# The gate's logits taken ahead of the squares of the value rows

## The chip, the cores and the metric

The kernel runs on one core of a Trainium2 chip. The core has five engines with instruction streams of their own, which meet only through semaphores: TensorE (PE, matrix products), VectorE (DVE), ScalarE (ACT), GpSimd (POOL) and SyncE (SP), whose queue issues nearly all DMA transfers. Each engine takes its instructions strictly in the order in which the program lists them. The metric is the device time of one execution in microseconds; the median of several executions counts.

## The reference

The result mixes two branches by a gate that is computed per token:

```python
x = A_u                                     # 1 x 2048 x 576
g = sigmoid((x * gate_w).sum(-1))           # the gate
a = _A_ref(x, ...)                          # a long convolution by spectra
b = _B_ref(x, w_q, k1, k2, u, v)            # product-key experts
return g * a + (1 - g) * b
```

Branch a builds a filter of 2048 taps for each of 576 channels from a state space of 128 modes and convolves it with x. Branch b scores 2048 tokens by 32 heads against two sets of 64 keys, takes the best two of each, and of their four sums the best two, weighs them with a softmax, and sums for each token the rows of `v` (4096 x 576) with weights `g * gelu(x . u)`.

## The kernel before

The products run in two half-precision parts: every large operand is split into a high and a low float16 part with a common scale, and three partial products are summed. For that the scale must be known first: for the value rows `v` it comes from the sum of their squares.

The program is written as generators, and a planner inside the kernel runs them. It keeps a clock of its own, `clock`, with estimated costs for each engine and for the DMA wire; a generator yields the time after which it wants to be called again, or waits with `ready(...)` until the planner believes that an operand is there. The planner only fixes the order of the instructions; on the chip each waits for what it really needs. So a generator that starts at another planned time, or in another order, changes the order of everything that is planned after it.

The stages, in order: the taps of the filter and, between them, the first scores (`s`, weights `whl`) and activations (`a`, weights `uhl`); `k_stage1`, the first transform of the 32 taps' rows (`k`, 32 pairs of output banks, evicted as `k1o` by ScalarE or VectorE and stored to `sk_d`, at most four tiles `k1o` in flight); `products`, the pointwise products of the spectra (`pr`, `pi`, `vf`, `pv`, `vo`); the last scores, `gating`, the transposes `tr`; the last activations; and then, token tile by token tile in the order 0, 15, 1, 14, ..., the one-hot products `S` (operands `A`, `Bg` from VectorE), their product with the activations' gelu (`gl`), the split of that into `wh`, and the output products `o` with the split value rows `vhl`. The products `s`, `a` and `k` run on the two row halves of the array, an upper and a lower half beside each other.

`v_norm` (L1529) is the generator around which the change lies. It reads 48 blocks of 128 rows through two buffers `vn`. The blocks 0 to 31 are the value rows: one DMA, and a sum of squares on ScalarE (`vj` with `vsum`). Behind block 31 the scale `sv` is formed and `vnormed` is set; `v_work` (L1577) waits for that, and then splits the eight chunks `vhl` of value rows: ScalarE writes the high part, and the low part goes to VectorE in one instruction or, where the planner thinks GpSimd free, over ScalarE and GpSimd. The raw rows of a chunk are loaded into the tile of the next one, so the tiles must be open. The blocks 32 to 47 are x itself: four DMAs (`au_load`), a multiplication by `gate_w` on GpSimd, and a sum on ScalarE (`vj` with `gA`). Behind the last a sigmoid makes the gate of `gA`, and `gates` is set.

`freq` (L1399) spawns `v_norm` 40 us of planned time after it has issued the loads of the spectra tables and taps (`tk`, `ksb`), opens the tiles of the chunks 0 to 2 behind `k_stage1`, of 3 and 4 behind `products`, and of 5 to 7 only when both `gated` (set by the last `gating`) and `gates` are set:

```python
        while not gated or not gates:
            yield 0.5
        FG.__exit__(None, None, None)
        WJ.__exit__(None, None, None)
        v_pool(5, 8)
```

All instructions of the three vector engines are recorded by one line, L136, the DMAs by L207 and the matmuls by L216, so the profile tells them apart by the names of their tiles.

Of the kernel before, what the change touches and what calls it, by code (L numbers as in the profile page):

```python
# [18 lines left out]
AF = mybir.ActivationFunctionType  # L19
# [121 lines left out]
def body(ctx: ExitStack, tc: tile.TileContext, xT, au, par, logdt, dskip, gatew, wq, kT, uT, vv,  # L141
# [56 lines left out]
    S = Engine(nc.scalar, rdy, clock, key, act_cost)  # L198
# [3 lines left out]
    def dma(o, i, q=None):  # L202
        t = max(clock[0], rdy.get(key(i), 0.0), queue[0])
        queue[0] = t + 0.45
        wire[0] = max(wire[0], t) + (2 if o.dtype in (F16, BF16) else 4) * o.shape[0] * size(o) / 3.4e5
        rdy[key(o)] = max(rdy.get(key(o), 0.0), wire[0] + 2.2)
        (q or DQ).dma_start(o, i)  # L207
# [63 lines left out]
    def spawn(gen, after=0.0):  # L271
        heapq.heappush(heap, (clock[0] + after, nseq[0], gen))
        nseq[0] += 1
# [118 lines left out]
    def au_load(a, t):  # L392
        for d, o in au_rows(au, t, a):
            dma(o, d)
# [53 lines left out]
    gA = top.tile([128, NT], F32, name="gA")  # L448
# [950 lines left out]
    def freq():  # L1399
        nonlocal ff, ab, iota_a, iota_b  # L1400
        ff = FG.__enter__()
        wrems.append(ff.tile([128, 2, 512], F16, name="wrem3"))
        ksb = KS.__enter__().tile([128, 4, NCK // 2, 32, 2 * NI], F16, name="ksb")
        fk = FK.__enter__()
        tabs = [fk.tile([128, 16, 2, 128], F16, tag="tk", name=f"tk{w0}", bufs=2) for w0 in (0, 16)]
        for w0, tkt in zip((0, 16), tabs):
            dma(tkt, tk_d[:, w0:w0 + 16, :])
        for j in range(4):
            while wire[0] > clock[0] + 2:
                yield 0.3  # L1410
            dma(ksb[:, j].rearrange("p c w i -> p c (w i)"),
                k_d[:, 32 * j:32 * j + 32].rearrange("c l z m n -> (l z m) c n"))
        spawn(v_norm(), 40)
        spawn(gating(0), 20)
        yield from k_stage1(ksb, fk, tabs)
        FK.__exit__(None, None, None)
        KS.__exit__(None, None, None)
        v_pool(0, 3)
        spawn(v_work())
        fp = FP.__enter__()  # L1420
        quota(sc=4, wb=5)
        yield 3
        yield from products(fp)
        FP.__exit__(None, None, None)
        quota(sc=4, wb=4)
        ab = ctx.enter_context(tc.tile_pool(name="ab", bufs=1, side="right"))
        iota_a = ab.tile([128, 128, 2], F16, name="iota_a")
        iota_b = ab.tile([128, 64, 2], F16, name="iota_b")
        V.tensor_copy(iota_a, cst[:, 384:512, None].to_broadcast([128, 128, 2]))
        V.tensor_copy(iota_b, cst[:, 512:576, None].to_broadcast([128, 64, 2]))  # L1430
        spawn(prep(0))
        v_pool(3, 5)
# [5 lines that stand above are left out]
        shut.append(1)  # L1438
# [87 lines left out]
    vhl, sv, vnormed, gates = [], [], [], []  # L1526
    vt = {}

    def v_norm():  # L1529
        ld = {}  # L1530

        def load(b):
            a = ff.tile([128, D], F32, tag="vn", name=f"vn{b}", bufs=2)
            if b < 32:
                dma(a, vv[128 * b:128 * b + 128])
            else:
                au_load(a, b - 32)
            ld[b] = a

        gw = row(gatew, "gw", ff)  # L1540
        load(0)
        for b in range(48):
            if b + 1 < 48:
                load(b + 1)
            a = ld.pop(b)
            yield from ready(a)
            ju = ff.tile([128, D], BF16, tag="ju", name=f"vj{b}")
            if b < 32:
                S.activation(ju, a, AF.Square, accum_out=vsum[:, b:b + 1])
            else:  # L1550
                G.tensor_mul(a, a, gw)
                yield from ready(a)
                S.activation(ju, a, AF.Copy, accum_out=gA[:, b - 32:b - 31])
            yield 2
            if b != 31:
                continue
            V.tensor_reduce(out=nut[:, 2:3], in_=vsum, axis=AX, op=OP.add)
            yield from ready(nut)
            tag = side()
            yield from need(tag)  # L1560
            p = bank(tag, "pvn")
            mm(p[:, 0:1], onesb, nut.bitcast(BF16)[:, 5:6], True, True, 0.05)
            yield from ready(p)
            sv.extend(root_scale(p[:, 0:1], 1.02))
            free(tag, sv[0], of=p)
            vnormed.append(1)
            del p
        S.activation(gA, gA, AF.Sigmoid)
        gates.append(1)

    def v_pool(c0, c1):

        vp = ctx.enter_context(tc.tile_pool(name=f"vp{c0}", bufs=1, side="right"))
        for c in range(c0, c1):
            vt[c] = vp.tile([128, 4, 2, D], F16, name=f"vhl{c}")
# [458 lines left out]
```

## Time and profile before

| | |
|---|---|
| median of 3 runs | 1461.31 us (1460.85 to 1463.2) |
| the profiled execution | 1463.78 us, of which the span is 1462.0 us |
| TensorE busy | 1426.9 us, 98% of the span |
| VectorE, ScalarE, GpSimd busy | 1199.1, 848.8, 527.5 us |
| granted TensorE clock, mean | 0.991 |
| sums of squares and of the gate on ScalarE (`vj`, 48) | first at 719.2 us, last at 969.9 us |
| sigmoid of the gate | 972.8 us |
| splits `vhl` on ScalarE | 859.7 to 1021.3 us |
| first output product `o` | 996.6 us |

A row of a timeline gives start and duration in us, engine, line, operation, output and inputs, the shape, a count, and in brackets how long the engine idled before and for what. A row of the slices gives the stretch, its length, the busy time of PE, weight load, DVE, ACT and POOL with the number of instructions, the granted TensorE clock (1.00 is full), the busy share of the DMA engines and GB/s. A row of the waits gives who waited for whom, the total in us, how often, and the longest.

### The profile page before, as it was taken

What the parts mean: (1) busy time and instruction counts of PE and PEld (TensorE: products, weight loads), DVE (VectorE), ACT (ScalarE), POOL (GpSimd) and SP (SyncE); (2) the same over time, 40 slices, a digit from 0 to 9 for tenths busy, and PEclk for the clock granted to TensorE, in tenths of its full rate; (3) what the DMA queues carried; (4) which work ended last, traced back from release to release, by engine and by line L of the source; (5) the groups of instructions that cost most, each with busy time, mean ns of one, the idle gap of its engine ahead of it and who ended that gap; (6) DMA issues with size and microseconds to landing.
All of it is one profiled execution on the core that took longest, in us unless ns stands there. A gap on an engine that the chain in (4) does not pass through costs nothing. (4 is left out here: it accounts for less than half of the span.)

```text
span 1462.0 us, 44130 instructions
## 1 busy us (share of the span) xinstructions
PE 1426.9 (98%) x17654; PEld 901.9 (62%) x17654; DVE 1199.1 (82%) x4559; ACT 848.8 (58%) x1477; POOL 527.5 (36%) x515
## 2 busy tenths in 40 slices
PE   7999999999999999999999999999899999999999
PEld 3465566554565565455654444446687887888787
DVE  6888699889889988767899997568998988998860
ACT  6647887987888877754566765755424224223310
POOL 0442266543472663430368899413110110010100
PEclk9999999999999999999999999999999999999999
DMA  9433543333341331248767786767433432442400
GB/s 312 124 112 101 160 126 113 109 122 107 112 147 47 126 103 45 74 146 258 252 253 254 271 287 213 243 195 251 146 101 117 140 120 91 133 148 67 156 10 17
DMA packets 134381, 215.89 MB, mean 148 GB/s; under 512 B 10912, under 2 KB 79904, under 8 KB 127776
## 3 DMA queue, kind: packets, MB, share of 16 engines
q1 hardware_dynamic: 134080, 213.01, 44.9%
q8 instruction: 138, 2.26, 0.6%
q14 instruction: 67, 0.55, 0.1%
q10 hardware_dynamic: 96, 0.07, 0.0%
HBM read 141.74 MB, written 71.30 MB: 146 GB/s over the span
## 5 line engine op out<-in xcount | busy, mean ns | idle before, releaser
L216 PE MATMUL s<-whl,xb 64*128 64x512 f16 x3072 | 466.0, 377 | 0.1
L216 PE MATMUL a<-xb,uhl 64*128 64x512 f16 (+1 forms) x3024 | 458.0, 378 | 0.7 <-ACT uhl L136 0.3
L216 PE MATMUL o<-vhl,wh 128*128 128x288 f16 x3072 | 390.1, 287 | 1.2 <-DVE vhl L136 1.2
L216 PEld LDWEIGHTS <-wh 128*128 128x128 f16 x3072 | 297.0, 98 | 79.5 <-issue 5.5
L216 PEld LDWEIGHTS <-xb 64*128 64x128 f16 x3456 | 222.1, 94 | 167.5 <-issue 14.8
L216 PEld LDWEIGHTS <-uhl 64*128 64x128 f16 (+1 forms) x3024 | 196.4, 94 | 167.0 <-issue 8.9
L136 ACT ACTIVATE wh<-gl,s_wg 128x1024 f16<-128x1024 f32 x64 | 68.9, 1137 | 199.0 <-DVE gl L136 199.0
L136 POOL TENSOR_TENSOR CS<-CS,ex 128x512 f32<-128x512 f32 x72 | 90.7, 1295 | 167.6 <-DVE ex L136 167.6
L136 POOL TENSOR_TENSOR ya<-ya,db 128x576 f32<-128x576 f32 x16 | 32.0, 2011 | 317.2 <-DMA ya<-in_au_dram 158.2
L216 PE MATMUL s<-wrem,xb 64*128 64x512 f16 x384 | 123.1, 376 | 0.0
L216 PE MATMUL a<-xb,wrem 64*128 64x512 f16 (+1 forms) x380 | 120.7, 377 | 0.0
L136 ACT ACTIVATE go<-a,i_a 128x512 f32<-128x512 f32 x100 | 68.4, 685 | 88.0 <-PE a L216 65.3
L136 DVE FIND_INDEX8 i<-m,sx 128x8 uint32<-128x64 f32 x592 | 116.5, 215 | 0.0
L136 DVE TENSOR_TENSOR gl<-S,gl 128x256 f32<-128x256 f32 x256 | 90.3, 414 | 16.4 <-PE S L216 10.0
L136 DVE SCALAR_TENSOR_TENSOR wh<-gl,s_wg,wh 128x1024 f16<-128x1024 f32 x64 | 89.6, 1428 | 14.2 <-ACT wh L136 14.1
L136 POOL TENSOR_TENSOR e<-aN,rt 128x512 f32<-128x512 f32 x72 | 84.0, 1189 | 47.4 <-PE kb L216 47.3
L136 DVE TENSOR_TENSOR Bg<-Be,vals 128x1024 f16<-128x1024 f16 x128 | 88.4, 732 | 2.2
L136 DVE FIND_INDEX8 i<-m,s 128x8 uint32<-128x64 f32 x432 | 87.0, 220 | 0.0
L136 DVE MAX8 m<-sx 128x8 f32<-128x64 f32 x592 | 81.4, 207 | 6.2 <-ACT sx L136 5.9
L136 ACT ACTIVATE gl<-gl 128x1024 f32<-128x1024 f32 x64 | 63.4, 1044 | 33.3 <-DMA gl<-g_d 33.2
L216 PE MATMUL S<-Bg,A 128*128 128x64 f16 x2048 | 74.6, 195 | 7.9 <-DVE Bg L136 7.9
L136 DVE MAX8 m<-s 128x8 f32<-128x64 f32 x432 | 61.7, 214 | 24.2 <-PE s L216 20.0
(209 smaller groups left out, 2468.3 us busy)
## 6 DMA issues: line engine op xcount, KB each, us to landing
g_d<-go SPq DMA_DIRECT2D x128, 256.0 KB, 2.6
gl<-g_d SPq DMA_DIRECT2D x32, 1024.0 KB, 5.4
wq<-in_wq_dram SPq DMA_DIRECT2D x16, 1152.0 KB, 6.1
su_d<-us SPq DMA_DIRECT2D x32, 288.0 KB, 2.6
sk_d<-k1o SPq DMA_DIRECT2D x32, 288.0 KB, 3.0
vn<-in_vv_dram SPq DMA_DIRECT2D x32, 288.0 KB, 5.2
ui<-su_d SPq DMA_DIRECT2D x16, 576.0 KB, 4.2
ki<-sk_d SPq DMA_DIRECT2D x16, 576.0 KB, 5.4
```

The lines of the kernel that those rows point to most:

```text
L136: return f(*a, **k)
L216: return T.matmul(o, l, r, start=start, stop=stop)
```

## The change

In `v_norm` the blocks are taken in the order 32 to 47, then 0 to 31; the sigmoid and `gates` stand behind block 47, the scale still behind block 31, which is now the last. `freq` spawns the generator 4 instead of 40 us of planned time after its own loads.

```diff
-        spawn(v_norm(), 40)
+        spawn(v_norm(), 4)
...
         gw = row(gatew, "gw", ff)
-        load(0)
-        for b in range(48):
-            if b + 1 < 48:
-                load(b + 1)
+        order = [*range(32, 48), *range(32)]
+        load(32)
+        for n, b in enumerate(order):
+            if n + 1 < 48:
+                load(order[n + 1])
             a = ld.pop(b)
...
             yield 2
+            if b == 47:
+                S.activation(gA, gA, AF.Sigmoid)
+                gates.append(1)
             if b != 31:
                 continue
...
-        S.activation(gA, gA, AF.Sigmoid)
-        gates.append(1)
```

The order of the instructions moves with it from the tap stage on. The first place is SP's queue at the start of `k_stage1`, behind the loads of the taps `ksb`; `k1o` with a number is the evicted tile of that tap, `vn32` and on are the blocks of x. Before:

```order
L207 DMA ksb_11201<-k_d_68 128x18x256 x3
L207 DMA sk_d_67<-k1o0_11703 32x4x576
L207 DMA sk_d_67<-k1o1_11706 32x4x576
L207 DMA sk_d_67<-k1o2_11758 32x4x576
L207 DMA sk_d_67<-k1o3_11772 32x4x576
L207 DMA sk_d_67<-k1o4_11827 32x4x576
L207 DMA sk_d_67<-k1o5_11840 32x4x576
```

and now:

```order
L207 DMA ksb_11201<-k_d_68 128x18x256 x3
L207 DMA gw_11647<-in_gatew_dram 128x576
L207 DMA vn32_11649<-in_au_dram 32x576 x4
L207 DMA vn33_11654<-in_au_dram 32x576 x4
L207 DMA sk_d_67<-k1o0_11715 32x4x576
L207 DMA vn34_11839<-in_au_dram 32x576 x4
L207 DMA sk_d_67<-k1o1_11718 32x4x576
L207 DMA sk_d_67<-k1o2_11772 32x4x576
L207 DMA vn35_11902<-in_au_dram 32x576 x4
L207 DMA sk_d_67<-k1o4_11851 32x4x576
L207 DMA sk_d_67<-k1o3_11787 32x4x576
```

Fourteen of the sixteen blocks of x, four DMAs each, and the row of `gate_w` now stand among the 32 stores of that stage, where that row and six value-row blocks, one DMA each, stood.

The second place is VectorE's order just ahead of its first work on the products `S15_0` of the second token tile (`gl15_0<-S15_0`). Before:

```order
L136 TENSOR_TENSOR Bg15_0_17192<-Be15_0_17190,vals_80 128x1024 x2
L136 TENSOR_TENSOR A115_1_17195<-iota_a_16322,vals_80 128x2048
L136 TENSOR_TENSOR Be15_1_17197<-iota_b_16323,vals_80 128x1024
L136 TENSOR_TENSOR Bg15_1_17199<-Be15_1_17197,vals_80 128x1024 x2
L136 SCALAR_TENSOR_TENSOR vhl4_16330<-vhl5_17144,sci_76,vhl4_16330 128x576 x2
L136 SCALAR_TENSOR_TENSOR vhl5_17144<-vhl6_17145,sci_76,vhl5_17144 128x576
L136 TENSOR_SCALAR go7_1_2_17422<-a7_1_2_17311,i_a_91 128x512
L136 TENSOR_SCALAR go7_2_3_17427<-a7_2_3_17277,i_a_91 128x512
L136 TENSOR_TENSOR gl15_0_17184<-S15_0_0_17388,gl15_0_17184 128x32x8
```

and now:

```order
L136 TENSOR_TENSOR Bg15_0_17228<-Be15_0_17226,vals_80 128x1024 x2
L136 TENSOR_TENSOR A115_1_17231<-iota_a_16476,vals_80 128x2048
L136 TENSOR_TENSOR Be15_1_17233<-iota_b_16477,vals_80 128x1024
L136 TENSOR_TENSOR Bg15_1_17235<-Be15_1_17233,vals_80 128x1024 x2
L136 SCALAR_TENSOR_TENSOR vhl6_16491<-vhl7_16492,sci_76,vhl6_16491 128x576
L136 SCALAR_TENSOR_TENSOR vhl7_16492<-vs_17160,sci_76,vhl7_16492 128x576
L136 TENSOR_SCALAR go7_2_3_17362<-a7_2_3_17278,i_a_91 128x512
L136 SCALAR_TENSOR_TENSOR vhl7_16492<-vs_17160,sci_76,vhl7_16492 128x576
L136 TENSOR_TENSOR gl15_0_17220<-S15_0_0_17383,gl15_0_17220 128x32x8
```

The last splits of value rows, of the chunks 6 and 7, now stand ahead of `S15_0`; before, the chunks 4 and 5 stood there.

The third place is VectorE's order later in the same passage, up to its first work on `S1_0` of the third token tile (`gl1_0<-S1_0`). Before:

```order
L136 SCALAR_TENSOR_TENSOR wh15_1_17662<-gl15_0_17184,s_wg_92,wh15_0_17661 128x1024
L136 SCALAR_TENSOR_TENSOR vhl6_17145<-vhl7_17146,sci_76,vhl6_17145 128x576
L136 SCALAR_TENSOR_TENSOR wh15_1_17662<-gl15_0_17184,s_wg_92,wh15_0_17661 128x1024
L136 SCALAR_TENSOR_TENSOR ya0_17523<-y0_0_0_17759,iuk_94,ya0_17523 128x288
L136 SCALAR_TENSOR_TENSOR ya0_17523<-y0_0_1_17764,iuk_94,ya0_17523 128x288
L136 SCALAR_TENSOR_TENSOR wh15_1_17662<-gl15_1_17185,s_wg_92,wh15_0_17661 128x1024
L136 SCALAR_TENSOR_TENSOR vhl7_17146<-vs_17540,sci_76,vhl7_17146 128x576
L136 SCALAR_TENSOR_TENSOR wh15_1_17662<-gl15_1_17185,s_wg_92,wh15_0_17661 128x1024
L136 SCALAR_TENSOR_TENSOR ya15_17528<-y0_1_0_17769,iuk_94,ya15_17528 128x288
L136 SCALAR_TENSOR_TENSOR ya15_17528<-y0_1_1_17774,iuk_94,ya15_17528 128x288
L136 SCALAR_TENSOR_TENSOR vhl7_17146<-vs_17540,sci_76,vhl7_17146 128x576 x2
L136 TENSOR_TENSOR gl1_0_17664<-S1_0_0_17826,gl1_0_17664 128x32x8
```

and now:

```order
L136 TENSOR_TENSOR A11_1_17657<-iota_a_16476,vals_80 128x2048
L136 TENSOR_TENSOR Be1_1_17659<-iota_b_16477,vals_80 128x1024
L136 TENSOR_TENSOR Bg1_1_17661<-Be1_1_17659,vals_80 128x1024 x2
L136 SCALAR_TENSOR_TENSOR wh15_1_17644<-gl15_0_17220,s_wg_92,wh15_0_17643 128x1024 x2
L136 SCALAR_TENSOR_TENSOR wh15_1_17644<-gl15_1_17221,s_wg_92,wh15_0_17643 128x1024 x2
L136 SCALAR_TENSOR_TENSOR ya0_17554<-y0_0_0_17751,iuk_94,ya0_17554 128x288
L136 SCALAR_TENSOR_TENSOR ya0_17554<-y0_0_1_17756,iuk_94,ya0_17554 128x288
L136 TENSOR_TENSOR gl1_0_17646<-S1_0_0_17777,gl1_0_17646 128x32x8
```

The splits of the chunks 6 and 7 have left this place, and the combinations of `ya15` stand further behind.

## Prediction

> **What bounds the kernel now.** I read the busy shares of the page first, then who TensorE waited for, then the span in slices of 10 us, then TensorE's timeline at the few gaps.
>
> ```profile
> PE 1426.9 (98%) x17654; PEld 901.9 (62%) x17654; DVE 1199.1 (82%) x4559; ACT 848.8 (58%) x1477; POOL 527.5 (36%) x515
> PE S L216 <- DVE Bg L136: 7.9, 6, 3.1
> PE k L216 <- ACT k1o L136: 2.4, 2, 2.2
> PE k L216 <- DVE m L136: 1.9, 1, 1.9
> PE tr L216 <- DVE vals L136: 1.2, 1, 1.2
> PE o L216 <- DVE vhl L136: 1.2, 1, 1.2
> ```
>
> TensorE (PE) is busy for 1426.9 of 1462.0 us, so all that a reordering can win is in 35 us of gaps. The change removes no matmul. What it can move is the waits listed (total us, times, longest), and these lie in two places: the stage of the tap transforms (`k`, 684 to 730 us) and the passage from the activations `a` to the one-hot products `S` and the output products `o` (915 to 1040 us). Slices of that passage (PE busy, PEld, DVE, ACT, POOL, then the granted clock):
>
> ```profile
> 920.00:930.00 10.00, 9.96 (x116) 5.60 (x117) 3.70 (x16) 6.88 (x19) 2.63 (x2) 0.66 0.92 306
> 950.00:960.00 10.00, 7.78 (x80) 3.63 (x78) 9.44 (x19) 3.05 (x7) 1.42 (x1) 0.83 0.35 95
> 1000.00:1010.00 10.00, 10.00 (x118) 8.18 (x117) 9.93 (x23) 2.40 (x4) 0.94 (x1) 0.84 0.76 204
> 1030.00:1040.00 10.00, 6.16 (x55) 4.43 (x55) 9.93 (x19) 0.42 (x1) 0.00 (x0) 0.70 0.01 2
> ```
>
> A gap costs twice: after it the granted clock falls. The same instructions at both clocks (start, duration, idle before):
>
> ```profile
> 920.04 0.31 PE L216 MATMUL tr<-identb,vals 128*64 128x64 bf16 x4 [1.23 <-DVE vals L136]
> 954.09 0.20 PE L216 MATMUL S<-Bg,A 128*128 128x64 f16 x1 [1.82 <-DVE Bg L136]
> 954.69 1.31 PE L216 MATMUL S<-Bg,A 128*128 128x64 f16 x31 [0.40 <-DVE Bg L136]
> 961.97 2.12 PE L216 MATMUL a<-xb,uhl 64*128 64x512 f16 x18
> 991.21 1.14 PE L216 MATMUL S<-Bg,A 128*128 128x64 f16 x32
> 999.24 0.19 PE L216 MATMUL S<-Bg,A 128*128 128x64 f16 x1 [1.75 <-DVE Bg L136]
> 1001.47 4.67 PE L216 MATMUL o<-vhl,wh 128*128 128x288 f16 x30
> 1015.86 2.15 PE L216 MATMUL y<-yz,tf 128*32 128x288 f32 x32
> 1017.94 3.85 PE L216 MATMUL o<-vhl,wh 128*128 128x288 f16 x30
> 1034.86 0.23 PE L216 MATMUL S<-Bg,A 128*128 128x64 f16 x1 [3.14 <-DVE Bg L136]
> 1035.46 1.81 PE L216 MATMUL S<-Bg,A 128*128 128x64 f16 x31 [0.37 <-DVE Bg L136]
> 1037.08 5.63 PE L216 MATMUL o<-vhl,wh 128*128 128x288 f16 x30
> ```
>
> 32 `S` take 1.14 us and 30 `o` 3.85 us at the full clock; behind the 3.14 us gap they take 1.81 and 5.63, some 2.5 us more.
>
> The Trainium skill, "TensorE: Matmul & The Clock Gate", section "HAM oscillation — how this bites in real kernels", says that only idle gaps above about 3.4 us cost clock. Here the trace differs: 1.23 us of idle stands ahead of a slice granted 0.66, 1.82 us ahead of none but within one granted 0.83. By the page the slow clock in the second term below (0.8 us) would be none of the wait's doing, and the sum 2.8 us instead of 3.6; I go by the rows.
>
> **The change, part by part.** *The squares' end and VectorE's part of the value rows.* The order of VectorE shows the remaining value-row splits (`vhl`) ahead of the first product of the second token tile, `S15_0`, where before six stood behind it, among the work on which `S15_2` and `S1_2` wait. Their prices, and what GpSimd adds to them:
>
> ```profile
> 1004.10 0.81 DVE L136 SCALAR_TENSOR_TENSOR vhl<-vhl,sci,vhl 128x576 f16<-128x576 f32 x1
> 1010.37 1.28 POOL L136 TENSOR_TENSOR vhl<-vhl,vhl 128x576 f16<-128x576 f32 x1 [9.43 <-ACT vhl L136]
> 1010.48 3.53 DVE L136 TENSOR_TENSOR Bg<-Be,vals 128x1024 f16<-128x1024 f16 x2
> 1018.45 2.16 POOL L136 TENSOR_TENSOR vhl<-vs,vhl 128x576 f16<-128x576 f32 x1 [3.19 <-ACT vs L136]
> 1019.39 1.83 DVE L136 SCALAR_TENSOR_TENSOR vhl<-vhl,sci,vhl 128x576 f16<-128x576 f32 x1
> 1028.63 0.93 DVE L136 SCALAR_TENSOR_TENSOR ya<-y,iuk,ya 128x288 f32<-128x288 f32 x2
> 1038.50 1.29 DVE L136 TENSOR_TENSOR Bg<-Be,vals 128x1024 f16<-128x1024 f16 x2
> ```
>
> VectorE was at 9.93 of 10 us in the slices at 1000 and 1030, so there it sets the pace. Gone from its chain between `S15_0` and `S1_2`: six splits at 0.81, 4.9 us; two `ya` combinations that now stand behind, 0.93; and the stretching of its instructions while GpSimd works on `vhl` (a `Bg` pair at 3.53 instead of 1.29, a split at 1.83 instead of 0.81; some of the first is due to another GpSimd instruction), of which I count half of 2.2 and the whole 1.0, 2.1 us. Together 7.9 us. But the order also draws `S1_2` forward: 156 `o` stand ahead of it instead of 192, 36 × 3.85/30 = 4.6 us less cover, against 8 more `a` matmuls, whose pair costs 2.12/9 = 0.24 at most and 0.22 from start to start: 0.9. Net 7.9 − 4.6 + 0.9 = 4.2 us of gain. Bounds: nothing, if the splits that moved forward make `S15_0` late instead (the slice at 920, with VectorE at 3.70 of 10, speaks against it), and 10 us, which is all that TensorE lost from `S15_0` at 991.2 to 1034.9 (43.7 us elapsed; 192 `o` at 0.123, six groups of `S` at 1.07, the 32 `y` at 2.1 and 14 `a` make 33.6).
>
> The Trainium skill, "SBUF — State Buffer", section "SBUF: two separate sides", says that VectorE and GpSimd share one port pair as an exclusive lock, the loser waiting out the whole instruction. By it the 1.28 and 2.16 us would return in full, 3.4 instead of my 2.1; the row of 3.53 us agrees with such a stop.
>
> *The first products.* Between `S0_1` and `S0_2` stand 50 `a` matmuls instead of 36: 14 × 0.11 = 1.5 us more cover for waits of 1.82 + 0.40, and with 0.7 us left I let the slow clock behind it go too (the slice at 950 was granted 0.83, 1.7 us of full clock less, and half of that fell on work: 0.8). Gain 2.3; bounds 0 and 3.3.
>
> *The transposes `tr`.* ScalarE no longer has four sums of the gate between its 16 evictions, but VectorE has four splits between them. 19 `a` instead of 11 lie between the transposes, 0.9 us of cover. I take 0.9 of the 1.23; bounds −2 (two of the split pairs on the path) and 4.6 (the wait and the clock of the slice at 920).
>
> *The gate's rows in the tap stage.* Sixteen blocks, each four loads, one multiplication on GpSimd, one sum on ScalarE, move from 842–970 us to behind the load of the taps; 14 of them are issued before the last of the 32 stores of `k1o`, on the same queue, SP. ScalarE runs its queue in order, and 50 of the 64 evictions `k1o` stand on it behind these sums. TensorE has four banks for them, two taps. What a late block does there, the squares showed, which until now began in this stage:
>
> ```profile
> 719.16 0.68 ACT L136 ACTIVATE vj<-vn 128x576 bf16<-128x576 f32 x1 [3.93 <-DMA vn<-in_vv_dram]
> 690.00:700.00 10.00, 9.78 (x120) 7.63 (x116) 5.97 (x42) 6.93 (x21) 2.40 (x8) 1.00 0.72 268
> 700.00:712.00 12.00, 11.98 (x143) 9.08 (x140) 11.09 (x85) 6.43 (x22) 4.18 (x14) 1.00 0.57 214
> 712.00:720.00 8.00, 6.51 (x76) 4.86 (x71) 6.08 (x37) 3.52 (x15) 3.85 (x13) 1.00 0.84 263
> 720.00:730.00 10.00, 9.23 (x101) 6.23 (x102) 8.72 (x60) 6.97 (x23) 1.13 (x4) 1.00 0.85 280
> L136 ACT ACTIVATE k1o<-k x50: 388/411/487, 686.3 to 729.6; 128x288 f32<-128x288 f32 x50
> L207 SPq DMA_DIRECT2D sk_d<-k1o x32: 517/518/1402, 687.0 to 730.0; - x32
> L207 SPq DMA_DIRECT2D vn<-in_au_dram x64: 310/419/1385, 842.1 to 963.7; - x64
> L136 POOL TENSOR_TENSOR vn<-vn,gw x16: 1399/1414/2385, 854.2 to 965.9; 128x576 f32<-128x576 f32 x16
> vn<-in_vv_dram SPq DMA_DIRECT2D x5, 288.0 KB, 4.6
> vn<-in_au_dram SPq DMA_DIRECT2D x22, 72.0 KB, 2.1
> ```
>
> From 712 to 730 us TensorE lost 18 − 15.74 = 2.3 us, and the first sum waited 3.93 us for its rows. That stall goes, since the squares now come after the stage. In its place: two buffers for the rows, so two blocks per round of four issues (4 × 0.42 = 1.7), landing (2.1 in a quiet window, 4.6 in this one), 1.41 on GpSimd and 0.68 + 0.19 on ScalarE: 6.1 to 8.6 us, 3.0 to 4.3 a block. Fourteen blocks in the 43.3 us of the evictions have 3.1 each. So the rows fall behind by up to 14 × 1.2 = 17 us at the worst landing and not at all at the best; the queue itself needs 32 × 0.52 + 56 × 0.42 = 40 of 43 us. I take a landing of 3.2 us, nearer the quiet row because the stage before the squares moved only 0.57 to 0.72 of the DMA time: 7.2 us a round, 0.5 a block over, 7 us in all, less the two taps of slack (2 × 1.4 = 2.8) at the end: about 4.2, against the 2.3 that goes. Cost 1.9. Bounds: a gain of 2.3, and a loss of 12 (17 − 2.8 − 2.3).
>
> *The stage of the products (730 to 915).* It loses 16 multiplications of 1.41 us on GpSimd and gets squares without any, and none of the waits listed at the top falls in it. I leave it at 0; bounds ±2, about what the squares' first block cost in the tap stage. The sigmoid moves ahead of two of the exponentials: as many table loads in the order as before, 43.
>
> *Pairs of row halves.* Counting the halves of the array in TensorE's order, 3684 pairs of full-height-split `s`, `a` and `k` matmuls stand instead of 3694, and 115 singles instead of 96: 9 more passes at 0.22, a cost of 1.9, which nothing hides, since TensorE is the bound.
>
> Sum: 4.2 + 2.3 + 0.9 − 1.9 + 0 − 1.9 = 3.6 us of gain. The profiled execution took 1463.78 us, 1462.0 of them span; it would become 1460.2. It stands 2.5 above the median of the runs, 1461.31, so for the median I say 1457.7, 0.25% faster. About 0.2%, 2.9 us, is what a measurement of this kernel can tell from no change.
>
> **The rivals.** *The tap stage is held by the gate's rows.* Speaks for it: SP at 40 of 43 us by issue alone, and a row that lands in 4.6 us under just this mixture. Against: the two quiet windows. It decides when a landing passes some 4 us: then a round is 8 us, a block 0.9 over, 12.6 in all, TensorE's loss 12.6 − 2.8 − 2.3 = 7.5 instead of 1.9, and the sum −2.0: 1463.3; at 4.6 us it is 1467.8. This is the side of slower.
>
> *The waits only change their place.* VectorE's work between 915 and 1037 us is not less by the change, two splits and three evictions `go` are even more in the order from the transposes to `S1_2`, some 4 us; where it was idle before (3.70 of 10 at 920) it can take them, but if it cannot, the 4.2 of the first term becomes 0.2 and the time 1461.7: no change.
>
> *More goes than I count.* If `tr` and both `S` waits vanish with their slow clock, the first three terms are 10 + 3.3 + 4.6 instead of 7.4, and the time is 1447; half of that is 1452.
>
> **How the numbers follow.** Forecast 0.38 and the larger gain 0.10; no change 0.24; the tap stage 0.28. Faster is 0.48, within 0.2% 0.24, slower 0.28. The forecast's own range is 1454 to 1460. The range for all reaches up to 1467, where the tap stage's bad landing ends, and down to 1450, and leaves out about 2 in 10.
>
> **What would show it.** Right: no wait of `S` on `Bg` above 2.5 us from 990 to 1040 and no `vhl` behind `S15_0` on VectorE; clock at 1030 to 1040 above 0.8. The tap stage: `k` waits for `k1o` above 5 us in total, ScalarE waiting for GpSimd's `vn`, last `k1o` later than 735. Wrong above all: a landing of the gate's rows above 4 us there, or a new wait of `S15_0`.

## The result, and the profile after

The changed kernel took 1460.52 us in the median of 14 runs (1458.07 to 1463.49), the kernel before 1462.12 (14 runs, 1458.90 to 1464.39). The ratio is 0.9991, with a 95% interval of 0.9981 to 1.0000: about a tenth of a per cent, and no change by the bound of 0.2%. The profiled execution took 1462.77 us (span 1461.0) against 1463.78 (span 1462.0) before.

The page of the changed kernel, and who TensorE waited for between 680 and 1100 us (total us, times, longest):

```profile
PE 1427.4 (98%) x17652; PEld 902.7 (62%) x17654; DVE 1196.3 (82%) x4573; ACT 837.1 (57%) x1452; POOL 520.7 (36%) x513
PE S L216 <- DVE Bg L136: 4.4, 6, 1.5
PE k L216 <- ACT k1o L136: 2.0, 4, 1.0
PE pr L216 <- DMA ki<-sk_d: 1.8, 1, 1.8
PE pv L216 <- DVE vo L136: 1.7, 1, 1.7
PE wn L216 <- ACT wj L136: 0.9, 1, 0.9
```

The waits of the late passage are nearly halved (`S` for `Bg` 7.9 to 4.4), those of `tr` and of `o` for `vhl` are gone. In their place stand waits that were not there before: `wn` and `pr` for `ki` at the start of the products, and `pv` at their end. (Before, `pi` and `pr` waited 0.9 us each at 886 to 896; these two are gone.) TensorE's timeline at these places (start, duration, idle before in brackets):

```profile
742.68 0.16 PE L216 MATMUL wn<-sc,onesb 64*128 64x1 bf16 x1 [0.75 <-DVE i L136]
743.97 0.16 PE L216 MATMUL wn<-sc,onesb 64*128 64x1 bf16 x1 [0.90 <-ACT wj L136]
750.89 0.43 PE L216 MATMUL pr<-ki,cst 64*64 64x256 f32 x2 [1.76 <-DMA ki<-sk_d]
...
913.16 1.08 PE L216 MATMUL pv<-vf,cst 64*64 64x256 f32 x4 [1.72 <-DVE vo L136]
963.74 0.20 PE L216 MATMUL S<-Bg,A 128*128 128x64 f16 x1 [0.36 <-DVE Bg L136]
965.41 1.10 PE L216 MATMUL S<-Bg,A 128*128 128x64 f16 x31 [1.48 <-DVE Bg L136]
...
995.57 1.14 PE L216 MATMUL S<-Bg,A 128*128 128x64 f16 x32
...
1003.68 0.20 PE L216 MATMUL S<-Bg,A 128*128 128x64 f16 x1 [1.37 <-DVE Bg L136]
...
1031.10 0.20 PE L216 MATMUL S<-Bg,A 128*128 128x64 f16 x1
1031.69 1.10 PE L216 MATMUL S<-Bg,A 128*128 128x64 f16 x31 [0.39 <-DVE Bg L136]
```

The first product of `S1_2`, which stood behind 3.14 us of idle time at 1034.86, now starts at 1031.10 without a wait (with 36 fewer `o` ahead of it). The slices (PE busy, PEld, DVE, ACT, POOL, granted clock, share of the transfer engines, GB/s; in the last three PE alone):

```profile
712.00:720.00 8.00, 7.02 (x82) 5.02 (x78) 5.37 (x43) 5.81 (x22) 5.88 (x12) 1.00 0.86 278
720.00:730.00 10.00, 9.28 (x107) 6.25 (x104) 7.82 (x50) 5.96 (x19) 6.10 (x14) 1.00 0.82 276
740.00:750.00 10.00, 7.36 (x117) 4.56 (x113) 8.54 (x69) 6.25 (x15) 2.97 (x7) 1.00 0.80 288
750.00:760.00 10.00, 9.11 (x111) 4.38 (x113) 8.08 (x34) 3.50 (x11) 4.93 (x7) 1.00 0.75 242
...
900.00:910.00 10.00, 10.00 (x138) 1.00 1.02 364
910.00:920.00 10.00, 8.28 (x54) 0.66 0.49 176
1030.00:1040.00 10.00, 9.61 (x128) 1.00 0.70 247
```

The two rows of the kernel before:

```profile
740.00:750.00 10.00, 9.75 (x178) 6.01 (x176) 8.45 (x58) 7.59 (x18) 6.09 (x9) 1.00 0.59 210
750.00:760.00 10.00, 10.00 (x106) 4.54 (x102) 9.92 (x68) 5.79 (x15) 9.16 (x16) 1.00 0.73 290
```

At 1030 TensorE is busy 9.61 of 10 us at the full clock (6.16 at 0.70 before). At 740 to 760 it lost 3.5 us (0.25 before); and the clock of 0.66 that stood behind the wait of `tr` at 920 now stands behind the wait of `pv`, one slice earlier.

In the tap stage the rows of the gate land quickly, and the stage is longer nevertheless:

```profile
L136 ACT ACTIVATE k1o<-k x52: 392/411/519, 687.8 to 734.8; 128x288 f32<-128x288 f32 x52
vn<-in_au_dram SPq DMA_DIRECT2D x47, 72.0 KB, 2.4
ACT vj L136 <- POOL vn L136: 6.9, 5, 2.3
```

The last `k1o` on ScalarE comes at 734.8 us instead of 729.6, though a row lands in 2.4 us; ScalarE waited 6.9 us for products of GpSimd.

### The profile page after: what moved, and what is told of

It is laid out like the page before. It is cut to its first block, busy times and chain, and to the rows that moved or that the text cites. A ratio compares the mean times of both kernels' runs of the same rounds, so it can differ in the third digit from the quotient of the medians.

```text
span 1461.0 us, 44118 instructions
## 1 busy us (share of the span) xinstructions
PE 1427.4 (98%) x17652; PEld 902.7 (62%) x17654; DVE 1196.3 (82%) x4573; ACT 837.1 (57%) x1452; POOL 520.7 (36%) x513
## 5 line engine op out<-in xcount | busy, mean ns | idle before, releaser
L216 PEld LDWEIGHTS <-xb 64*128 64x128 f16 x3456 | 226.5, 94 | 167.5 <-issue 14.5
L136 DVE FIND_INDEX8 i<-m,s 128x8 uint32<-128x64 f32 x520 | 104.8, 221 | 0.0
L136 DVE FIND_INDEX8 i<-m,sx 128x8 uint32<-128x64 f32 x504 | 99.3, 217 | 0.0
L136 DVE MAX8 m<-s 128x8 f32<-128x64 f32 x520 | 74.2, 214 | 26.5 <-PE s L216 22.5
L136 DVE TENSOR_TENSOR A<-iota_a,vals 128x2048 f16<-128x2048 f16 x64 | 78.4, 1224 | 0.0
L136 ACT ACTIVATE CS<-CS 128x1024 f32<-128x1024 f32 x72 | 74.6, 1050 | 6.3 <-DVE CS L136 6.1
```

The lines of the kernel that those rows point to most:

```text
L136: return f(*a, **k)
L216: return T.matmul(o, l, r, start=start, stop=stop)
```

## The experiments

My theory after the result: the late passage gained about what was forecast, and the gain was spent in four places: the gate's rows in the tap stage, the start of the products, the end of the products (the loads of the value rows beside the stores `z_d`), and fewer pairs of row halves. The rival: the gain was never there, since VectorE has as much to do as before, and waits only changed place. All runs are compared with the kernel before on the same chip; the median of the kernel before lay between 1461.2 and 1462.1 throughout.

**Six splits less, nothing else moved.** In the kernel before, in its own order:

```diff
-                        V.scalar_tensor_tensor(h[:, j, 1, :], x, sv[0], h[:, j, 0, :], op0=OP.mult, op1=OP.subtract)
+                        if 12 <= len(nsplit) < 18:
+                            V.charge("scalar_tensor_tensor", h[:, j, 1, :], x, sv[0], h[:, j, 0, :], op0=OP.mult, op1=OP.subtract)
+                            nc.vector.memset(h[:, j, 1, :], 0.0)
+                        else:
+                            V.scalar_tensor_tensor(h[:, j, 1, :], x, sv[0], h[:, j, 0, :], op0=OP.mult, op1=OP.subtract)
+                        nsplit.append(1)
```

`charge` tells the planner the cost of the split, so that the order stays; the kernel leaves out the low parts of six blocks of value rows.

> The kernel before, in exactly its order, with six of VectorE's nine splits between S15_0 and S1_2 turned into a fill of the same half tile (their values are left out; 0.81 us each and up to 1.8 beside POOL becomes a fill that reads nothing). This does alone what the largest term of the prediction said of the change. If VectorE's chain sets the end of this passage: the waits of S for Bg, 17 us in six before by sum with clock, fall by 4 us or more and the time is 1456 to 1458.5. If the time removed from VectorE there is only waited for elsewhere (the arrival of loads, ScalarE's copies, the order of TensorE): 1460 to 1462, and the waits change place.

1459.48 us, ratio 0.9981 (0.9971 to 0.9990): faster, with a median between the two expectations. The fills, and three starts of `S`: the first row of `S` is that of `S15_0`, the last that of `S1_2`:

```profile
L1616 DVE MEMSET vhl<- x6: 298/298/298, 978.6 to 1016.8; 128x288 uint32 x6
...
989.03 1.14 PE L223 MATMUL S<-Bg,A 128*128 128x64 f16 x32
...
997.08 0.19 PE L223 MATMUL S<-Bg,A 128*128 128x64 f16 x1 [1.76 <-DVE Bg L136]
...
1031.45 0.20 PE L223 MATMUL S<-Bg,A 128*128 128x64 f16 x1 [3.14 <-DVE Bg L136]
```

Only three of the six fills lie in the passage (at 1002.0, 1004.0 and 1016.8). The other three stand at 978.6 to 979.5, ahead of `S15_0`, and behind them VectorE has nothing to do for 9.7 us. So the run removes less than its expectation says. From `S15_0` to `S1_2` TensorE takes 1031.45 − 989.03 = 42.42 us instead of 43.65, which is 1.2 us less; from VectorE's first eviction `gl` of `S15_0` to `S1_2` it is 40.8 instead of 42.0, also 1.2 less. What VectorE is relieved of there arrives at TensorE one to one. So the passage is paced by VectorE, as the prediction had it, but this run shows it for 1.2 us and not for the 4.2 forecast.

`S1_2` starts 3.4 us earlier than before (1034.86 to 1031.45), but 2.2 of these were there at `S15_0` already (991.21 to 989.03), ahead of all that the fills could do. Most of that is the clock: the slice from 950 to 960, granted 0.83 before, is granted 1.00 here behind the same waits. Of the 2.5 us between the medians the traces place 1.2; where the rest lies is open.

My expectation of the waits was wrong. `S` waits 7.9 us for `Bg` as before, and 3.14 ahead of `S1_2` as before; what went is the wait of `o` for `vhl`, 1.2 us. (The 17 us that the expectations give to the waits of `S` before stand in no view; the waits shown above are 7.9.) A relief of the pacing engine need not show in the wait one looks at.

**Each half of the change alone.** The early start with the old order:

```diff
-        spawn(v_norm(), 40)
+        spawn(v_norm(), 4)
```

> The first half of the change alone: the generator of the value rows starts at +4 instead of +40, and the squares stay ahead of the gate's rows, as before. The splits left for VectorE between S15_0 and S1_2 are nine, as before (three after the change), and 225 products of a row half stand alone (184 before, 205 after). If the saving in the late passage comes from the smaller number of splits there: the waits of S for Bg stay near the 17 us of before, and the time is 1461.5 to 1464. If an early start of the rows is enough (the rival that only the time of the squares counts): under 9 us of waits of S and 1458 to 1460.5.

1471.98 us, ratio 1.0075 (1.0060 to 1.0089). Neither expectation had this time. `S` waited 6.7 us for VectorE (2.2 for `Bg`, 4.5 for `ya`), against 7.9 for `Bg` before, so the early norm relieved the late passage by little. And the loads of the value rows now fell at 793 us, into the middle of the products:

```profile
800.00:810.00 10.00, 6.02 (x68) 2.59 (x60) 8.85 (x52) 2.74 (x5) 9.28 (x9) 1.00 1.04 376
810.00:820.00 10.00, 8.08 (x76) 3.27 (x76) 1.59 (x9) 6.45 (x19) 5.61 (x8) 0.66 0.67 202
...
811.92 1.12 PE L216 MATMUL pv<-vf,cst 64*64 64x256 f32 x4 [5.90 <-ACT vo L136]
...
ACT vo L136 <- DMA z_d<-vo: 6.9, 1, 6.9
```

Two loads of 1.2 MB fill the transfer engines (share 1.04), a store `z_d` on the same queue lands after up to 12.0 us (median 4.1), ScalarE cannot refill `vo` for 6.9 us, and TensorE stands for 5.9 us, with a clock of 0.66 behind it. It is the wait of `pv` of the changed kernel, more than three times as long.

The new order with the old start:

```diff
-        spawn(v_norm(), 4)
+        spawn(v_norm(), 40)
...
-        while not gated or not gates:
+        while not gated or not gates or not vnormed:
```

The second line opens the last tiles of `vhl` only behind the squares.

> The second half alone: the gate's rows ahead of the squares, and the start left at +40 (the last tiles of vhl are opened only when the squares are done, because this order would otherwise close the pool of the rows under them). Tap stage: no gate's row falls in it, so its last k1o copy comes back to about 730 us (734.8 after the change). Late passage: the sum of the squares comes at about 970 instead of 890, all splits go behind the products, 72 products o stand ahead of S1_2 instead of 156. If the order alone carried the gain: 1458 to 1460. If it needs the early start, since the splits now all lie in the passage of S: waits of S over 15 us, 1463 to 1475.

1502.32 us, ratio 1.0277 (1.0263 to 1.0291): the direction as expected, the size not by far. With the last square at 958 us all splits lie behind the products; TensorE waits 24.3 us for `Bg` alone, and 8.2 of it at once:

```profile
PE S L216 <- DVE Bg L136: 24.3, 15, 8.2
...
1032.89 0.23 PE L216 MATMUL S<-Bg,A 128*128 128x64 f16 x1 [8.19 <-DVE Bg L136]
```

The two halves are not two changes whose effects add (+10.5 and +40.9 us alone against −1.6 together): the time at which the norm is known decides what its loads and splits run beside (the first loads go out at 793, 897 and 969 us).

**The gate's rows.** A third buffer, with every queue and engine in the same order:

```diff
-            a = ff.tile([128, D], F32, tag="vn", name=f"vn{b}", bufs=2)
+            a = ff.tile([128, D], F32, tag="vn", name=f"vn{b}", bufs=3)
```

> The changed kernel with three buffers instead of two for the rows that pass POOL; every engine and every queue has exactly the same order. If the two buffers' loop (load 2.4 us, product on POOL, copy on ScalarE) holds the tap stage after the change: ScalarE's wait for POOL's products falls from 7.0 us to under 3, the last k1o copy comes 3 us or more earlier than 734.8, and the time is 1456.5 to 1459. If the tap stage is held by the order in which the copies k1o and vj alternate on ScalarE and by the stores sk_d, not by the buffers: last k1o within 1.5 us of 734.8 and 1459.5 to 1461.5, no difference to the change as it stands.

1459.48 us, ratio 0.9989 (0.9977 to 1.0002): no difference to the change as it stands.

```profile
L136 ACT ACTIVATE k1o<-k x52: 392/410/493, 687.0 to 734.0; 128x288 f32<-128x288 f32 x52
...
ACT vj L136 <- POOL vn L136: 7.6, 6, 2.5
```

The last `k1o` comes 0.8 us earlier and ScalarE waits for GpSimd as long as in the change. The loop of two buffers does not hold the stage. One thing in this profile matters below: with the same rows in the same order, no wait of `pr` for `ki` is listed, `pv` waits 0.8 us instead of 1.7, and the slice from 910 to 920 is granted 1.00.

Then the rows themselves, cut to 64 of 576 columns, in the order of the changed kernel:

```diff
-                G.tensor_mul(a, a, gw)
+                G.less("tensor_mul", 64, a, a, gw)
                 yield from ready(a)
-                S.activation(ju, a, AF.Copy, accum_out=gA[:, b - 32:b - 31])
+                S.less("activation", 64, ju, a, AF.Copy, accum_out=gA[:, b - 32:b - 31])
...
```

`less` works on 64 columns and charges the planner for 576; the four loads of a row block are cut in the same way. The gate is then a sum over 64 columns only.

> The changed kernel, in exactly its order, with the gate's rows cut to 64 of 576 columns in load, product and copy (the gate's values are left out of the computation so far). It prices the gate's rows where the change put them. If they cost the tap stage and the start of the products what the trace of the change suggests (3.3 us of TensorE between 730 and 760): last k1o copy back to 731 or less (734.8), TensorE 29 of 30 us in 730 to 760, and 1456 to 1458. If the stage is longer because of the new order of the products and copies, not of the rows' work: last k1o copy after 733 and 1459.5 to 1461.

1455.43 us, ratio 0.9955 (0.9941 to 0.9969): the sixteen blocks of rows cost 5.1 us where the change puts them, or somewhat more, since a ninth of their columns and all their instructions are still there.

```profile
PE 1424.4 (98%) x17654; PEld 903.7 (62%) x17654; DVE 1196.7 (82%) x4573; ACT 830.4 (57%) x1452; POOL 504.4 (35%) x513
...
L136 ACT ACTIVATE k1o<-k x52: 392/411/429, 686.2 to 732.1; 128x288 f32<-128x288 f32 x52
...
740.00:750.00 10.00, 8.44 (x135) 4.63 (x133) 8.32 (x56) 5.83 (x16) 2.34 (x8) 1.00 0.71 247
750.00:760.00 10.00, 9.45 (x123) 4.75 (x121) 9.43 (x51) 5.86 (x16) 8.21 (x10) 1.00 0.74 267
```

The time is even below the first expectation; its details came only in part: the last `k1o` comes at 732.1, halfway back to 729.6, and TensorE gets back 1.4 of the 3.5 us lost from 740 to 760. What goes is the wait of `pr` for `ki` (1.76), whose rows are stored last in the tap stage. But that wait is absent from the three-buffer run too, with all the rows in place, so the rows alone do not make it. The waits of `wn` stay (0.67 and 0.89), so they belong to the new order and not to the rows. The 5.1 us are shown by the times; the trace can't point them all out. The mean clock of this profile is also higher, 0.998 to 0.995, which of 1461 us is 4.4 us of full clock, and the 3.0 us by which TensorE is busy less are within that.

**The loads of the value rows at the products' end.** Three trials on the wait of `pv`. First, the loads let go when the gate is done:

```diff
-            while not vnormed or c not in vt or (c < 7 and c + 1 not in vt):
+            while not gates or c not in vt or (c < 7 and c + 1 not in vt):
                 yield 1
...
+            while not vnormed:
+                yield 1
             h = vt[c]
```

> The changed kernel, with the loads of the first two blocks of value rows (2.4 MB) let go as soon as the gate's sigmoid is done, in the middle of the products, instead of when the norm is known at about 905. If these loads delay the products' last stores z_d at 908 to 913 and so make the wait of pv for vo (1.72 us) and the low clock of 910 to 920 (0.66): both go, TensorE's idle and slowed time there falls by 3 to 5 us, of which 1.4 are lost to 14 more lone products of row halves: 1457 to 1459.5. If the stall at the end of the products has another cause (the copies of vo queue behind the splits on VectorE): it stays, and the time is 1460 to 1462.5.

1462.93 us, ratio 1.0011 (1.0001 to 1.0021). The wait of `pv` went, and the clock at 910 to 920 is 1.00; but the kernel is 2.4 us slower than the change by the medians. So neither expectation holds as a whole: the stall and the clock went as the first has it, and the time is above both. The planner had made another order from it, in which TensorE is busy for 1430.5 us instead of 1427.4.

Second, the same loads issued from ScalarE's queue:

```diff
-            dma(raw[c], vv[r:r + 512].rearrange("(k p) d -> p k d", p=128))
+            dma(raw[c], vv[r:r + 512].rearrange("(k p) d -> p k d", p=128), nc.scalar if c < 2 else None)
```

> The changed kernel, in its order, with the loads of the first two blocks of value rows (1.2 MB each) issued from ScalarE's queue instead of SyncE's. If the products' last stores z_d are late because they lie behind these loads in one queue: the stores z_d land in about 3 us again, the wait of pv for vo (1.72 us) and the clock of 0.66 go, 1457 to 1459. If it is the engines of the transfers that are full (busy share 1.02 at 900 to 910), the queue makes no difference: z_d lands as late, pv waits 1 us or more, 1459.5 to 1462.

1465.47 us, ratio 1.0015 (1.0002 to 1.0028), and 5 us above the change by the medians (3.5 by the two ratios): worse than either expectation.

```profile
905.64 0.27 PE L216 MATMUL pr<-ui,cst 64*64 64x64 f32 x2 [1.99 <-DMA ui<-su_d]
...
900.00:910.00 10.00, 6.39 (x86) 2.65 (x83) 4.90 (x10) 3.37 (x8) 7.51 (x11) 0.92 1.01 382
```

The stores `z_d` land sooner (a median of 3.5 us instead of 4.6 over the five around there) and the wait of `pv` is gone, but TensorE now waits for the operands `ui` and `ki`, which stand ahead of the loads when all are on SP's queue, and it loses 3.6 us in this slice instead of 1.7 in the next. What is full are the 16 transfer engines (share 1.01, 382 GB/s), not the queue; that the loads took their share ahead of the operands is how I read it, since with one queue `ui` was not late. The Trainium skill, "DMA: Bandwidth & Descriptors", section "Queues, rings and completion order", has each transfer engine alternate between the queues that have work, packet by packet; the run agrees, with `ui` 2.0 us late beside loads issued from the other queue.

Third, the loads at 780 us, with three row buffers and an order that differs from that of the three-buffer run in 72 rows of TensorE. VectorE's order differs more (4567 instructions in the profile instead of 4573, ScalarE 1465 instead of 1452), so it isn't only the place of the loads that is tried:

```diff
-            while not vnormed or c not in vt or (c < 7 and c + 1 not in vt):
+            while not (vnormed or len(vrows) >= 20) or c not in vt or (c < 7 and c + 1 not in vt):
...
+            while not vnormed:
+                yield 1
```

> The changed kernel with three row buffers (as in vn3) and the first two loads of value rows let go after 20 rows, at about 770, instead of behind the norm at 890. The order of TensorE differs from vn3 in 72 rows of 26,294, and the number of passes of row halves is the same (4082), so nothing but the place of the loads is tried. If the collision of these loads with the products' last stores costs the wait of pv and the low clock after it: both go (pv waits under 0.3 us, clock 1.00 in 910 to 920) and the time is 1 to 3 us under vn3's 1459.5, so 1456.5 to 1458.5. If that wait and the clock are made up for later anyway, or the loads now hit the start of the products (ui and ki): 1459 to 1462.

1461.15 us, ratio 0.9991 (0.9981 to 1.0001), against 0.9989 for the run with three buffers alone: no gain, as the second expectation said, though not for its reason. No wait at 911 any more, but one of `pv` where the loads now lie (slices with PE alone):

```profile
780.00:790.00 10.00, 9.94 (x119) 1.00 1.00 365
790.00:800.00 10.00, 8.51 (x89) 0.94 1.01 367
...
PE pv L216 <- ACT vo L136: 1.5, 1, 1.5
```

What these 2.4 MB cost TensorE depends on the few microseconds in which they meet the products' stores: nothing at 852 us in the kernel before (from 850 to 870 share 1.00 to 1.04, TensorE busy throughout) and no wait of `pv` at 768 in the first trial, 1.5 us at 780, 1.7 at 897 (0.8 there with three buffers), 5.9 at 793.

**The order itself.** Starts at +24 and at +6 (the latter with three buffers, alone and with early loads):

```diff
-        spawn(v_norm(), 4)
+        spawn(v_norm(), 24)
...
-        while not gated or not gates:
+        while not gated or not gates or not vnormed:
```

> The changed kernel with the start of the value rows at +24 instead of +4: the rows come behind much of the tap stage, the planner leaves 181 products of a row half alone (205 after the change, 184 before) in 4070 passes instead of 4082, and seven splits on VectorE between S15_0 and S1_2 (three after, nine before). If lone halves and the tap stage are what ate the gain: 2 to 3 us for each, less 3 for the four splits, so 1457 to 1459.5. If the early start itself carries the gain, since the norm must be known before the products end: the norm comes at about 915 to 925 instead of 890, and the time is 1465 or more.

1464.76 us, ratio 1.0015 (1.0006 to 1.0025). This is close to the second expectation (1465 or more), and the last square is at 922.7 us, in the stretch named there; the waits of `S` for `Bg` are back at 7.2 us.

```diff
-        spawn(v_norm(), 4)
+        spawn(v_norm(), 6)
...
-            a = ff.tile([128, D], F32, tag="vn", name=f"vn{b}", bufs=2)
+            a = ff.tile([128, D], F32, tag="vn", name=f"vn{b}", bufs=3)
```

> The changed kernel with three row buffers and the start of the rows at +6 instead of +4: 193 products of a row half stand alone (vn3 205, before 184), 4076 passes instead of 4082; five splits on VectorE between S15_0 and S1_2 instead of three. From the runs so far the busy time of TensorE at one clock grows by about 0.17 us for each product that stands alone more. If that holds: TensorE's busy time 2 us under vn3's 1426.2 at the same mean clock (1424), and the time 1458 to 1460, as two more splits take up to 1.6. If lone products cost nothing beyond a pass of 0.22 us each: busy 1425 to 1426 and 1459.5 to 1462.

1464.33 us, ratio 1.0018 (1.0008 to 1.0028). Both expectations missed. With 12 lone halves fewer, TensorE was busy for 1426.7 us and not for 1424, but its mean clock was also lower, 0.994 to 0.995, which is some 1.5 us. So the price of 0.17 us for a lone half, put together from earlier runs, is not borne out, and not refuted either. A start later by two of the planner's units cost 4 to 5 us against the same kernel at +4, with waits that neither expectation had:

```profile
PE S L216 <- DVE Bg L136: 6.8, 5, 3.2
PE tr L216 <- DVE vals L136: 2.4, 1, 2.4
```

> Both together, as a version that may beat both kernels: start at +6, three row buffers, the first two loads of value rows let go after 28 rows; 191 products of a row half stand alone, 4075 passes. If the wait of pv and the lone products are separate costs, the gains add: 1456 to 1458.5. If the order of the late passage that follows eats them (S waits for Bg again over 7 us): 1459.5 to 1462.

1461.28 us, ratio 0.9997 (0.9987 to 1.0007), as the second expectation said: `S` waits 7.3 us for `Bg`. No version tried that computes everything beats the change by more than can be measured.

The last run was therefore the kernel before with a shift that should mean nothing:

```diff
-        spawn(v_norm(), 40)
+        spawn(v_norm(), 39)
```

> The kernel before with the start of the value rows at +39 instead of +40, and nothing else: a shift that means nothing for any stage, but from which the planner makes another order (192 products of a row half alone instead of 184, 4076 passes instead of 4072, seven splits on VectorE between S15_0 and S1_2 instead of nine). If the fine order of the plan is itself worth as much as the change under study: the time differs from before by 2 us or more, to either side (about 1458 to 1460 if the two splits carry it at 0.8 to 1.8 each, 1463 to 1466 if new waits come up, as in the kernel started at +6). If only the named terms count: less 1.6 for two splits, plus 1 for four passes, so 1460.5 to 1462.5, no difference.

1463.62 us, ratio 1.0015 (1.0003 to 1.0027). It is the first expectation, on its slower side. One unit of start time, with two splits fewer in the passage, moves the time by 0.15% (0.03 to 0.27), which is of the size of the change under study (0.09%, 0 to 0.19), and to the other side. The profiled execution of this kernel, 1459.99 us, is one of its shortest, so what made the others longer its trace can't show.

## Why the prediction was right or wrong

The time forecast was 1457.7 us and came out at 1460.5, inside the range and in the case "no change", to which I gave 0.24. The likeliest case, 0.25% faster, had the time 2.8 us too low and the gain 2.0 us too large (3.6 against 1462.1 − 1460.5 = 1.6). Three steps failed: the second wait in the first products, the products' stage at zero, and the mechanism of the gate's rows. It was not the rival of the case "no change" that came true: its mechanism, that VectorE cannot take the splits earlier, is refuted by the passage below. All three signs named for a right forecast are there: no wait of `S` from 990 to 1040 is longer than 1.4 us, no split stands behind `S15_0`, and the clock from 1030 to 1040 is 1.00.

That the time is near is in part luck, and the two profiles show how. In both the stage of the taps begins at the same time (the first row is the kernel before, the second the change):

```profile
L216 PE MATMUL k<-ksb,tk x256: 279/282/293, 684.5 to 728.6; 64*128 64x288 f16 x128
L216 PE MATMUL k<-ksb,tk x256: 279/282/441, 684.5 to 731.8; 64*128 64x288 f16 x128
```

`S15_0` follows at 991.2 us before and at 995.6 after, and the span ends at 1462.0 and 1461.0. Eight `a` (0.9 us) lie behind `S15_0` that lay ahead of it. So the change loses 4.4 + 0.9 = 5.3 us ahead of `S15_0`, where the terms of the forecast add to a loss of 0.6 (2.3 + 0.9 − 1.9 − 1.9). Behind it the change gains 5.4 + 0.9 = 6.3, where the forecast had 4.2. Two errors stand against each other. These are one execution each: the three-buffer run, with the same order, comes to `S15_0` 2.9 us earlier than the change.

By the row experiment the change without the cost of the gate's rows is 6.5 us faster than before; the prediction had 7.8 (3.6 and the 4.2 that it charged for the rows). The rows took back 5.1 us instead of 4.2. Their cost where they stood before was not measured.

*VectorE's chain, 4.2 us: right in mechanism, and near in size.* From `S15_0` to `S1_2` the trace of before has 1034.86 − 991.21 = 43.65 us, the trace after 1031.10 − 995.57 = 35.53. Of these 8.1 us, 36 `o` (4.6) only stand behind, and 8 `a` (0.9) are more: 4.4 us gained. The six-splits run shows by itself that VectorE paces this passage, at 1.2 us of effect; the rest of the 4.4 is read from the two traces. The other 1.9 of the 6.3 us lie behind `S1_2`. There the prediction had itself read off some 2.5 us of slow clock behind the gap, and left them out of its sum.

*The first products, 2.3 us: failed.* The 14 `a` covered the first wait (1.82 to 0.36), but the second grew from 0.40 to 1.48. VectorE's `Bg` pair took longer because a split of GpSimd now ran beside it:

```profile
962.98 2.38 DVE L136 TENSOR_TENSOR Bg<-Be,vals 128x1024 f16<-128x1024 f16 x2
...
963.15 1.66 POOL L136 TENSOR_TENSOR vhl<-vhl,vhl 128x576 f16<-128x576 f32 x1 [8.23 <-ACT vhl L136]
```

The pair takes 1.29 alone. In the two profiles together 9 of the 256 `Bg` products take more than 0.8 us, and beside each of them a GpSimd instruction runs. The splits that left the later passage are not gone; one of them now meets `Bg` here. I counted GpSimd's disturbance where it went away and not where it came to. Of 2.3 us 0.4 of waiting were had, and the slow clock behind the first wait, which had come in the profile of before, did not come; but it did not come in the six-splits run either, with the waits of before, so that is no merit of the change. The Trainium skill, "SBUF — State Buffer", section "SBUF: two separate sides", describes this as an exclusive lock of a port pair, and the added 1.1 us agrees with a stop for most of GpSimd's instruction.

*The transposes, 0.9 us.* The wait of 1.23 went, but the 1.72 us of `pv` stand 7 us ahead of where it was, with a clock of 0.66 behind them. In this profile no gain is left. I had put the stage of the products at zero because none of the waits listed lay in it, and did not follow the norm's later time to its loads: the change moves their 2.4 MB from 852 us, where they cost TensorE nothing, to 897, where they delay the last stores; with them at another place or in another queue, the wait of `pv` went (first two trials). The bound of ±2 contains the wait but not the clock behind it.

*The gate's rows, 1.9 us net: the sign right, the mechanism wrong.* The term was made from the landing of the loads in a loop of two buffers. The landing was 2.4 us, better than the 3.2 I took, and a third buffer changes nothing. From 712 to 730 TensorE won 0.6 of the 2.3 us I gave for the squares' stall, and in 740 to 760 it lost 3.5 where before it lost 0.25: in this profile the stage's cost is less in stalls within it than at its end, where the last `k1o` comes 5 us later and `ki`, read from its stores, holds up the products' first `pr`, beside the waits of `wn` that came with the new order. I had charged the stage's own gaps, and not who waits for its last store. How much of the 5.1 us goes by this path is open, since the wait for `ki` is also absent from the three-buffer run, which is no faster than the change. A further part has no term in the forecast: the clock right at the stage's start, 0.72 from 684 to 690 in the change and with three buffers, 1.00 before and in the row experiment, is some 1.7 us. It is not shown to be the rows' doing: the run of the new order at +40, without the rows there, has 0.72 too. Of the signs that I named for the rival, ScalarE's wait for GpSimd's `vn` came (6.9 us) and the last `k1o` came close (734.8); `k` waited only 2.0 us for `k1o`, and the condition (a landing above 4 us) did not come, so it was the wrong point to decide by.

*Pairs of row halves, 1.9 us.* In profiles of the same mean clock, 0.995, TensorE is busy for 1427.4 us in the change and 1426.2 with three buffers, but for 1423.5 in the six-splits run, which has the order of before, and 1423.2 at +39, whose order is near it:

```profile
PE 1423.5 (98%) x17654; PEld 908.5 (62%) x17654; DVE 1200.4 (82%) x4559; ACT 848.9 (58%) x1477; POOL 525.7 (36%) x515
```

So 3 to 4 us of TensorE's time are lost in the order, in two profiles of each kind, more than the 1.9 charged. That single halves are its cause is not shown: the run at +6 has 12 fewer, but a lower clock, and does not decide it. (The expectations of the runs count 205 singles instead of 184 and 4082 passes instead of 4072, where the prediction had 115 instead of 96 and 9 passes more; by passes the two nearly agree.) What else makes TensorE's work longer in that order stays open.

## What to carry to other kernels

A change that moves work earlier moves its loads as well: ask which stage they now share the transfer engines with, which stores of that stage come late, and who waits for their buffers. Count a disturbance (GpSimd beside VectorE) at the new place as well as at the old. Where a planner writes the order, make a meaningless shift of one unit and measure it before believing a gain of a few tenths of a per cent: here it was worth 0.15% (0.03 to 0.27). And read a run's trace from its start: a place that comes earlier may have been earlier already ahead of the edit.

## What the hardware showed that I had not expected

Loads issued from ScalarE's queue instead of SyncE's did not relieve the transfer engines but delayed transfers of the other queue: TensorE waited 2.0 us for `ui`, for which it had not waited at all. And the length of a gap of TensorE did not set the fall of the clock behind it. The granted clock was 0.66 in the slice with the gap of 1.72 us and 0.66 in the one with the gap of 5.90. The gaps of 1.82 and 0.40 us ahead of the first products stood in a slice granted 0.83 in the kernel before and, with 1.82 and 0.39, in one granted 1.00 in the six-splits run, in the same order. So a slow clock read behind a gap in one profile is no price that the next execution must pay.
